# A 1 KB read of w_in on ScalarE's DMA queue at the start of an attention and feed-forward kernel

## The chip, the cores and the metric

The kernel runs on one NeuronCore of a Trainium2 chip, as one launch. Its time is device microseconds (us), lower is better. Five engines work side by side, each with its own instruction stream: TensorE (PE in the profile, with its weight loads as PEld), VectorE (DVE), ScalarE (ACT), GpSimd (POOL) and SyncE (SP). Transfers between the chip's main memory and SBUF are done by 16 DMA engines; an instruction on one of the five engines' queues starts each transfer, and "landing" is the moment at which all of it has arrived and whoever waits for it may go on.

## The reference

```python
def _attn_ref(x, state):                       # x 8x8x512x64, state 8x8x32x64
    scores = scale * x @ state^T ; a = softmax(scores) ; xread = a @ state
    scores2 = scale * state @ x^T ; a2 = softmax(scores2) ; sread = a2 @ x
    return concatenate([xread, sread], axis=2)
def _moe_ref(x, w_in, w_out):                  # 4608 rows of 512, w_in 512x2048, w_out 2048x512
    h = x @ w_in
    g = h - tanh(h)
    return g @ w_out
```

The output of the attention, 8 batches of 544 rows with the heads side by side, is the input of the feed-forward layer. Both weights come as 64-bit floating-point numbers and are turned into 32-bit ones on the chip.

## The kernel before

The heads' states are small (32 rows), so the kernel multiplies them into w_in ahead of time: for every batch and every head it forms state times w_in, and the hidden layer is then one product of the softmax weights with that. The 512 tokens of a batch and the 2048 hidden units are worked through in 16 steps of 128 hidden units per batch. One step is a product into a bank of PSUM (`hps`), tanh on ScalarE, subtraction on VectorE, a split into a high and a low part (ScalarE casts, VectorE subtracts), and the products with w_out into four banks (`ops`). This steady state makes up the time from about 60 us on.

Before it stands a start-up stage, in which the weights aren't there yet. It is written by hand: three strings list, for PE, DVE and ACT, the order of the steps by letters, and nothing on these engines may overtake. In it, the first batch's scores and softmax are computed, and each block of w_in, as soon as it has landed, is converted: `Weight.steps` (lines 146 to 161) gives for one block two shifts and masks on VectorE (L157, L158), a scaling copy on ScalarE (L160) and a last addition on VectorE (L161). Then `product` multiplies it with the states (L826).

A block of w_in or w_out is 128 rows of 4 KB, 512 KB in all, and `Weight.load` starts its transfer on SyncE's queue (L144; L135 for blocks that are kept in pairs). In DRAM the 16 blocks of w_in lie behind each other. The blocks are called `w00d`, `w01d`, `w02d` and so on as they land. The other inputs of the start-up lie in one array, `in_early`, which `fetch` (L657) takes piece by piece: `head` (states and a quarter of the tokens of the first heads, 384 KB), `xT00` (256 KB), `xT01` (512 KB), `sps` (256 KB), `sp4` (256 KB), `bdr1` (64 KB) and `xT1` (two of 512 KB).

All transfers of the kernel before are started by SyncE, in program order. Which come first is written out at L660 to L670: `head`, `xT00`, `w00d`, `xT01`, `sps`, `w01d`, `sp4`, `bdr1`, `xT1` twice, and then 14 weight blocks. Completions are counted on eight semaphores, which are called DMAHW0 to DMAHW7 and given out in turn; a transfer isn't started until the one eight places ahead, which used the same semaphore, has landed.

Of the kernel before, what the change touches and what calls it, by code (L numbers as in the profile page):

```python
# [10 lines left out]
U32 = mybir.dt.uint32  # L11
# [34 lines left out]
def attention_ffn(ctx: ExitStack, tc: tile.TileContext, early, xT, xn, bh, sm, sl, win, wout, xout, sout):  # L46
# [10 lines left out]
    nc = tc.nc  # L57

    cpool = ctx.enter_context(tc.tile_pool(name="cpool", bufs=1))
    pool = ctx.enter_context(tc.tile_pool(name="pool", bufs=2))  # L60
# [593 lines left out]
    def fetch(dst):  # L654
        nonlocal start
        n = dst.shape[-1]
        nc.sync.dma_start(dst, early[P * start : P * (start + n)].rearrange("(p n) -> p n", p=P))  # L657
        start += n

    fetch(head[:, :768])  # L660
    fetch(xb.rearrange("p c x -> p (c x)"))
    load(1)
# [481 lines left out]
```

## Time and profile before

| | us |
|---|---|
| median of 3 runs | 640.93 |
| lowest and highest run | 639.73 and 642.14 |
| span of the profiled execution, first to last instruction | 638.7 |
| PE busy in it | 631.7 (99%) |
| DVE busy in it | 438.4 (69%) |
| ACT busy in it | 353.6 (55%) |

For the profiled execution its span is known; the runs' median stands 2.2 us above it, which is what lies around the span and the spread of the runs. The profile gives for each instruction its engine, line, start and length, and for an idle stretch ahead of it what ended it. A DMA's own row (SPq) is the time in which the queue starts it, not the transfer.

### The profile page before, as it was taken

What the parts mean: (1) busy time and instruction counts of PE and PEld (TensorE: products, weight loads), DVE (VectorE), ACT (ScalarE), POOL (GpSimd) and SP (SyncE); (2) the same over time, 40 slices, a digit from 0 to 9 for tenths busy, and PEclk for the clock granted to TensorE, in tenths of its full rate; (3) what the DMA queues carried; (4) which work ended last, traced back from release to release, by engine and by line L of the source; (5) the groups of instructions that cost most, each with busy time, mean ns of one, the idle gap of its engine ahead of it and who ended that gap; (6) DMA issues with size and microseconds to landing.
All of it is one profiled execution on the core that took longest, in us unless ns stands there. A gap on an engine that the chain in (4) does not pass through costs nothing.

```text
span 638.7 us, 10135 instructions
## 1 busy us (share of the span) xinstructions
PE 631.7 (99%) x3772; PEld 502.4 (79%) x3772; DVE 438.4 (69%) x752; ACT 353.6 (55%) x639; POOL 0.3 (0%) x5
## 2 busy tenths in 40 slices
PE   8999999999999999999999999999999999999998
PEld 4476867888888788878888788878888788888887
DVE  5998898898683874688563678377764766464563
ACT  4966677787783443656553458254543453343553
POOL 0000000000000000000000000000000000000000
PEclk9999999999999999999999999999999999999999
DMA  8993897477885335543633236682463124221410
GB/s 331 401 304 116 316 352 244 139 241 233 247 258 155 104 99 201 172 137 107 196 113 105 79 111 208 209 308 83 136 194 90 35 83 148 76 66 34 132 34 33
DMA packets 66592, 105.84 MB, mean 166 GB/s; under 512 B 12272, under 2 KB 32368, under 8 KB 66544
## 3 DMA queue, kind: packets, MB, share of 16 engines
q1 hardware_dynamic: 66544, 105.21, 50.4%
q8 instruction: 29, 0.48, 0.3%
q14 instruction: 19, 0.16, 0.1%
HBM read 69.01 MB, written 35.65 MB: 164 GB/s over the span
## 4 chain that ended last, share of the span: by engine, by line
PE 94%; DVE 2%; DMA 2%; ACT 1%; issue 0%; SPq 0%; DVEq 0%
PE ops L566 19%; PE ops L567 19%; PE ops L568 19%; PE hps L513 8%; PE hps L515 8%; PE hps L514 8%; PE hps L498 2%; PE mps L249 2%; PE hps L887 1%; DMA w01d<-in_win 1%; PE mps L826 1%; PE rps L436 1%; PE sps L318 1%; PE hps L499 1%; PE mps L248 1%; PE ops L913 1%
## 5 line engine op out<-in xcount | busy, mean ns | idle before, releaser
L566 PE MATMUL ops<-wo,g 128*128 128x512 f32 x534 | 209.0, 393 | 0.0
L567 PE MATMUL ops<-wo,g 128*128 128x512 f32 x534 | 208.3, 390 | 0.0
L568 PE MATMUL ops<-wo,g 128*128 128x512 f32 x534 | 198.7, 390 | 0.0
L527 ACT ACTIVATE t<-hps 128x512 f32<-128x512 f32 (+1 forms) x119 | 70.7, 595 | 145.9 <-PE hps L515 143.0
L527 DVE TENSOR_TENSOR t<-hps,t 128x512 f32<-128x512 f32 (+1 forms) x119 | 81.4, 685 | 99.7 <-ACT t L527 99.2
L566 PEld LDWEIGHTS ops<-wo,g 128*128 128x128 f32 x534 | 100.3, 188 | 26.0 <-issue 2.9
L567 PEld LDWEIGHTS ops<-wo,g 128*128 128x128 f32 x534 | 100.2, 188 | 21.9 <-issue 1.3
L568 PEld LDWEIGHTS ops<-wo,g 128*128 128x128 f32 x534 | 99.8, 188 | 22.3 <-issue 0.8
L116 DVE TENSOR_TENSOR g<-t,g 128x512 fp32r<-128x512 f32 (+1 forms) x134 | 87.2, 655 | 33.6 <-ACT g L115 32.5
L115 ACT CAST g<-t 128x512 fp32r<-128x512 f32 (+1 forms) x134 | 79.6, 596 | 45.7 <-DVE t L527 39.2
L513 PE MATMUL hps<-aT,m 128*128 128x512 f32 x232 | 90.6, 391 | 0.0
L514 PE MATMUL hps<-aT,m 128*128 128x512 f32 x232 | 90.3, 389 | 0.0
L515 PE MATMUL hps<-aT,m 128*128 128x512 f32 x232 | 89.9, 390 | 0.0
L513 PEld LDWEIGHTS hps<-aT,m 128*128 128x128 f32 x232 | 43.5, 188 | 10.8 <-DVE w31r L158 0.8
L515 PEld LDWEIGHTS hps<-aT,m 128*128 128x128 f32 x232 | 43.5, 188 | 9.2
L514 PEld LDWEIGHTS hps<-aT,m 128*128 128x128 f32 x232 | 43.6, 188 | 8.9
L116 DVE TENSOR_TENSOR wst<-w,wst 64x512 fp32r<-64x512 f32 (+1 forms) x56 | 36.3, 648 | 8.1 <-ACT wst L115 6.5
L116 DVE TENSOR_TENSOR m<-mr,m 128x1024 fp32r<-128x1024 f32 x29 | 35.4, 1222 | 3.5 <-ACT m L115 3.0
L250 ACT COPY st<-mps 128x512 f32<-128x512 f32 (+1 forms) x56 | 30.2, 557 | 10.1 <-PE mps L249 6.8
L115 ACT CAST m<-mr 128x1024 fp32r<-128x1024 f32 x29 | 30.4, 1047 | 5.7 <-DVE mr L282 5.5
L115 ACT CAST wst<-w 64x512 fp32r<-64x512 f32 (+1 forms) x56 | 32.8, 585 | 0.7
L498 PE MATMUL hps<-srT,wm 128*128 128x512 f32 x60 | 21.7, 396 | 0.0
(232 smaller groups left out, 575.2 us busy)
## 6 DMA issues: line engine op xcount, KB each, us to landing
md<-st SPq DMA_DIRECT2D x96, 128.0 KB, 3.0
mr<-md SPq DMA_DIRECT2D x20, 512.0 KB, 4.1
xn<-in_xn SPq DMA_DIRECT2D x16, 512.0 KB, 6.1
out_x<-ob SPq DMA_DIRECT2D x30, 256.0 KB, 3.0
xT<-in_xT SPq DMA_DIRECT2D x12, 512.0 KB, 5.2
w<-wf SPq DMA_DIRECT2D x12, 512.0 KB, 4.1
pd<-pe SPq DMA_DIRECT2D x16, 256.0 KB, 2.3
p2t<-pd SPq DMA_DIRECT2D x64, 64.0 KB, 2.0
```

The source lines that it names most:

```text
L115: nc.scalar.copy(hi, src)
L116: return (sub or nc.vector).tensor_sub(lo, src, hi)
L249: nc.tensor.matmul(ps, s[:, 0, h], t[:, e], start=(g == 1), stop=True)
L250: nc.scalar.copy(stage[:, e], ps)
L498: nc.tensor.matmul(ps, mhi[k][:, cols], both, start=(k == 0), stop=False)
L513: nc.tensor.matmul(ps, mhi[k][:, cols], ahi[:, k], start=(k == 0), stop=False)
L514: nc.tensor.matmul(ps, mhi[k][:, cols], alo[:, k], start=False, stop=False)
L515: nc.tensor.matmul(ps, mlo[k][:, cols], ahi[:, k], start=False, stop=(k == 1))
L527: tanhs.append((nc.scalar.activation(t, ps, AF.Tanh).ins, nc.vector.tensor_sub(t, ps, t).ins))
L566: nc.tensor.matmul(o, g[:, 0, tok], wo[f][:, 0, cols], start=first, stop=False)
L567: nc.tensor.matmul(o, g[:, 0, tok], wo[f][:, 1, cols], start=False, stop=False)
L568: return nc.tensor.matmul(o, g[:, 1, tok], wo[f][:, 0, cols], start=False, stop=last).ins
```

## The change

One small transfer is added. It reads, from the first block of w_in (the one that lands as `w00d`), the first 64 bytes of each of the first 16 rows, which are 4 KB apart, into a tile of 16 partitions by 64 bytes. The tile, `touch`, is read by nothing. The instruction stands on ScalarE's queue, in the program ahead of all other transfers.

```diff
         nc.sync.dma_start(dst, early[P * start : P * (start + n)].rearrange("(p n) -> p n", p=P))
         start += n
 
+    touch = pool.tile([16, 16], U32, tag="touch", name="touch", bufs=1)
+    nc.scalar.dma_start(touch, win[0].bitcast(U32)[:16, :16])
+
     fetch(head[:, :768])
     fetch(xb.rearrange("p c x -> p (c x)"))
     load(1)
```

On ScalarE, at the start of the program, the row of instructions before is this; `s` is the copy of the first scores, `w00r` the scaled copy of the first weight block, and in brackets stand the semaphores waited for:

```order
0 L1139 UNCONDITIONAL_BRANCH [waits barrier_Pool_Activation_PE_DVE_SP_release]
1 L723 ACT_TABLE_LOAD
2 L723 COPY s_197<-sps_175 128x256 [waits DVE_49]
3 L724 COPY s_197<-spsb 128x256 [waits DVE_49]
4 L160 ACTIVATE w00r<-w00d 128x512 [waits DMAHW2_49]
```

And of the changed kernel:

```order
0 L1142 UNCONDITIONAL_BRANCH [waits barrier_Pool_Activation_PE_DVE_SP_release]
1 L661 DMA touch<-in_win 16x16
2 L726 ACT_TABLE_LOAD
3 L726 COPY s_199<-sps_177 128x256 [waits DVE_49]
4 L727 COPY s_199<-spsb 128x256 [waits DVE_49]
5 L160 ACTIVATE w00r<-w00d 128x512 [waits DMAHW3_49]
```

The new transfer stands ahead of the load of ScalarE's table, and it has taken the first of the eight semaphores, so that `w00d` now counts on the fourth.

On SyncE's queue, from its start to the first weight block that waits, before:

```order
1 L657 DMA head<-in_early 128x768
2 L657 DMA xT_128<-in_early 128x512
3 L144 DMA w00d<-in_win 128x1024
4 L657 DMA xT_129<-in_early 128x1024
5 L657 DMA sps<-in_early 128x512
6 L144 DMA w01d<-in_win 128x1024
7 L657 DMA sp_127<-in_early 128x512
8 L657 DMA bdr_125<-in_early 128x128
9 L657 DMA xT_130<-in_early 128x1024 [waits DMAHW0_49]
10 L657 DMA xT_130<-in_early 128x1024 [waits DMAHW1_49]
11 L144 DMA w02d<-in_win 128x1024 [waits DMAHW2_49]
```

And of the changed kernel:

```order
1 L657 DMA head<-in_early 128x768
2 L657 DMA xT_128<-in_early 128x512
3 L144 DMA w00d<-in_win 128x1024
4 L657 DMA xT_129<-in_early 128x1024
5 L657 DMA sps<-in_early 128x512
6 L144 DMA w01d<-in_win 128x1024
7 L657 DMA sp_127<-in_early 128x512
8 L657 DMA bdr_125<-in_early 128x128 [waits DMAHW0_49]
9 L657 DMA xT_130<-in_early 128x1024 [waits DMAHW1_49]
10 L657 DMA xT_130<-in_early 128x1024 [waits DMAHW2_49]
11 L144 DMA w02d<-in_win 128x1024 [waits DMAHW3_49]
```

The order of the transfers is the same. One wait is new: `bdr1` (bdr_125) is now started only once `touch` has landed. The later ones wait for the same transfers as before, on the next semaphore. On PE, DVE and POOL the order doesn't change.

## Rows read from the trace of the kernel before

**Rows 1.** Stretches: from:to us, length, busy time by engine, clock, DMA share, GB/s.

```profile
8.00:48.00 40.00, 37.34 (x523) 22.59 (x522) 39.53 (x67) 31.32 (x61) 0.00 (x0) 1.00 1.04 363
48.00:60.00 12.00, 11.57 (x73) 7.92 (x74) 11.10 (x18) 7.07 (x11) 0.00 (x0) 1.00 0.38 129
60.00:638.70 578.70, 575.70 (x3157) 467.51 (x3155) 386.18 (x667) 313.18 (x564) 0.00 (x0) 1.00 0.47 152
```

**Rows 2.** The chain that ended last, at the start: start us, us, what.

```profile
3.06 8.17 DMA w01d<-in_win
...
11.25 0.68 ACT w01r L160
```

**Rows 3.** Timeline of PE, DVE and ACT, first 10 us: start, us, engine, line, operation.

```profile
0.73 1.28 ACT L723 ACT_TABLE_LOAD   x1 [0.73 <-PEq L1130]
...
3.74 1.12 PE L707 MATMUL sps<-head 128*64 128x256 f32 x4
4.65 1.07 PE L718 MATMUL spsb<-xT,head 128*64 128x256 f32 x4
...
5.39 0.37 ACT L723 COPY s<-sps 128x256 f32<-128x256 f32 x1 [3.38 <-DVE e L733]
...
6.25 0.69 DVE L743 TENSOR_REDUCE m<-e 128x16 f32<-128x512 f32 x1
...
8.03 0.43 DVE L157 TENSOR_SCALAR w<-w00d 128x512 uint32<-128x512 uint32 x1 [1.10 <-DMA w00d<-in_win]
8.03 0.68 ACT L160 ACTIVATE w00r<-w00d 128x512 int32<-128x512 uint32 x1 [1.41 <-DMA w00d<-in_win]
...
9.32 1.08 PE L710 MATMUL sps<-xT,head 128*64 128x512 f32 x4 [1.27 <-DMA xT<-in_early]
```

**Rows 4.** Stretches of the first 8 us, columns as in the first group.

```profile
0.00:4.00 4.00, 3.12 (x8) 2.11 (x10) 0.00 (x0) 1.28 (x1) 0.30 (x5) 1.00 0.54 184
4.00:5.00 1.00, 1.00 (x6) 0.46 (x6) 0.09 (x1) 0.00 (x0) 0.00 (x0) 1.00 0.84 313
5.00:6.00 1.00, 1.00 (x5) 0.36 (x2) 0.59 (x2) 0.37 (x1) 0.00 (x0) 1.00 0.90 266
6.00:7.00 1.00, 1.00 (x4) 0.84 (x4) 0.90 (x2) 0.37 (x1) 0.00 (x0) 1.00 0.86 317
7.00:8.00 1.00, 1.00 (x5) 0.57 (x3) 0.00 (x0) 0.00 (x0) 0.00 (x0) 1.00 1.06 412
```

**Rows 5.** DMA issues: tiles, queue, count, KB each, median us to landing.

```profile
sr<-sx SPq DMA_DIRECT2D x32, 16.0 KB, 1.9
...
ob<-half SPq DMA_DIRECT2D x4, 256.0 KB, 3.0
...
w00d<-in_win SPq DMA_DIRECT2D x1, 512.0 KB, 6.4
...
smr<-in_sl SPq DMA_DIRECT2D x1, 256.0 KB, 3.0
```

**Rows 6.** Timeline of SyncE's queue: start us, us of starting the transfer, line.

```profile
0.73 0.39 SPq L657 DMA_DIRECT2D head<-in_early  x1
...
1.64 0.43 SPq L144 DMA_DIRECT2D w00d<-in_win  x1
...
4.29 1.25 SPq L657 DMA_DIRECT2D bdr<-in_early  x1
5.58 1.20 SPq L657 DMA_DIRECT2D xT<-in_early  x2
8.03 0.33 SPq L144 DMA_DIRECT2D w02d<-in_win  x1
9.29 0.33 SPq L135 DMA_DIRECT2D wo0d<-in_wout  x1
```

**Rows 7.** Timeline of ACT and DVE where the block wo2 has landed.

```profile
25.30 1.19 ACT L188 ACTIVATE wo2r<-wo2d 128x1024 int32<-128x1024 uint32 x1 [0.81 <-DMA wo2d<-in_wout]
25.45 0.68 DVE L186 TENSOR_SCALAR wor<-wo2d 128x1024 uint32<-128x1024 uint32 x1
```

## The prediction

> **What bounds the kernel now.** I first looked at the long stretches. From 60 us to the end PE is busy 575.70 of 578.70 us [rows 1]: nothing in there can be won by a small transfer at the start, but whatever makes that stretch begin earlier is won whole, since PE then simply has its work earlier. Ahead of it, from 8 to 48 us, VectorE is busy 39.53 of 40 us and PE 37.34 [rows 1]. So VectorE's list of steps, once it has begun at 8 us, runs almost without a gap, and a start that is earlier by some part of a us ends earlier by the same, unless one of its inputs isn't there. So the question is what starts that list and which inputs hold it.
>
> The chain of waits says what comes first: a transfer, w01d, which holds the chain from 3.06 us for 8.17 us, and then ScalarE's conversion of it at 11.25 us [rows 2]. The timeline shows the same one block earlier. VectorE ends the maximum at 6.25 + 0.69 = 6.94 us and then idles 1.10 us until w00d has landed, at 8.03 us; ScalarE waits 1.41 us for the same landing, and PE waits 1.27 us for xT01, which is the next in the queue, until 9.32 us [rows 3]. So the start-up is held by landings, and w00d is the first that is waited for.
>
> **Why w00d lands so late.** It is started at 1.64 us [rows 6] and takes 6.4 us to land [rows 5]. Is it only the bytes? To 4 us 4 x 184 = 736 KB (of 1000 bytes) came, to 5 us 1049, to 6 us 1315 [rows 4]. In the queue stand head, xT00 and w00d with 384 + 256 + 512 KB (of 1024), which is 1180. So as many bytes as these three have were in at 5 + 131 / 266 = 5.5 us. The same for head and xT00 (655): before 4 us, and PE works on xT00 at 4.65 us [rows 3], at most 0.9 us after its bytes. By that w00d would land at 6.4 us; it landed at 8.03. Some of the 16 engines were 1.6 us late with their share of it, while others were already at later transfers. And from 4 to 7 us the rate was 313, 266 and 317 GB/s, against 412 right behind [rows 4]: 99 + 146 + 95 = 340 KB less than at the full rate, or 340 / 412 = 0.83 us of all engines. Something stalls engines in that stretch. It may be the first reads of w_in; this is what a touch ahead could take away. It may also be load.
>
> **The change part by part.** *The instruction itself* stands ahead of the table load on ScalarE. No transfer of before is started there; on SyncE starting one took 0.33 to 1.25 us [rows 6], and I take 0.4. The table load now ends at 2.01 us, and ScalarE's next work is at 5.39 us after 3.38 us of idling [rows 3]. With 0.4 us, or even 1.25, nothing is late: cost zero, hidden by that idling.
>
> *The transfer* is 16 x 64 bytes, 1 KB beside the 736 KB of the first 4 us. Its nearest row is the 16 KB transfer, which lands after 1.9 us [rows 5]. If the first read of w_in is slow it could take as long as w00d, 6.4 us. So it lands between 2.6 and 7.1 us; I take 3, nearer to the small row.
>
> *The new wait* holds bdr1 on SyncE, and behind it both xT1 and the weight blocks from w02d on. bdr1 was started at 4.29 us [rows 6], after my 3 us, so the cover is 1.3 us. At the late end bdr1 starts at 7.1 us instead, but by 4.29 us transfers of 2.75 MB (all up to sp4) had been handed over and 0.8 MB had come [rows 4]; the remaining 1.9 MB takes 4.7 us at 412 GB/s, until 9 us, so the DMA engines don't run dry either. Cost zero at both ends. The later transfers wait for the same predecessors as before.
>
> *The gain* lies between nothing and what VectorE idles. If w00d landed at 6.4 us, VectorE could go on at 6.94 us rather than at 8.03: 1.09 us. But that isn't kept. At 25.30 us ScalarE has waited 0.81 us for wo2d, and VectorE takes the same block at 25.45 us [rows 7]. VectorE is thus only 0.15 us behind that landing: if its list comes 1.09 us earlier, it stands still there until wo2d is in. What passes is 0.15 us and whatever wo2d itself lands earlier. That is a matter of bytes, since the DMA engines are full from 7 us on (412 GB/s, share 1.06 [rows 4]; 1.04 as a mean of 8 to 48 us [rows 1]): if no stall of w_in's first reads is left, the bytes missing in w00d's own stretch come back, 99 + 0.49 x 146 = 171 KB or 0.41 us. So the gain is between 0 and 0.56 us. I take 0.3, the middle: there is a late w00d, which speaks for some gain, but no row that says that its lateness is a first read. The sum: 638.7 - 0.3 = 638.4 us of span, and 640.93 - 0.3 = 640.6 us.
>
> For the other side there is a row too: in_sl is first read by a transfer of 256 KB that lands after 3.0 us, and a read of 256 KB of an array that the kernel itself wrote shortly before (ob<-half) takes 3.0 us as well [rows 5]. There the first read costs nothing that can be seen.
>
> The Trainium skill has two places that speak against the change. *DMA: Bandwidth & Descriptors*, section "Issuing engines are not separate DMA queues", says that transfers started by ScalarE and SyncE run on the same 16 engines and interleave, so that a second queue saves only the time of starting. *HBM Reference*, section "Latency", gives an average access as 0.2 us and one under high load as 2 us; w00d's lateness of 1.6 us would by that be load, which a touch doesn't take away. By either the sum would be 640.9; no run so far tells these from a slow first read.
>
> **The rivals.**
>
> *Nothing moves.* The stall at 4 to 7 us is load, or 64 KB of addresses are too few to prepare a block of 512 KB, or the touch waits in the same engines in which head follows, so that the wait is only moved. w00d then lands at 8.03 us again, and the time is 640.9 us. For it speaks in_sl's row [rows 5], against it that the stall begins just as w00d's turn comes.
>
> *The whole stall goes.* Everything missing from 4 to 7 us comes back (0.83 us), wo2d lands by as much earlier and VectorE keeps 0.15 + 0.83 = 0.98 us: 640.0 us. Against it: a good part of the missing bytes falls in the time from 5.5 us on, when xT01 of another array is in turn.
>
> *The stall moves to the front, and it is slower.* The touch arrives at the 16 engines together with head. If the wait for w_in's first reads stops an engine, head's rows stand behind it. head comes first in the chain: PE begins at 3.74 us with it, and the maximum on VectorE ends at 6.94 us, with 1.09 us to spare before w00d [rows 3]. A delay of head decides from 1.09 us on. With the 1.6 us of w00d's lateness the maximum ends at 8.5 us, VectorE goes on 0.5 us later than now, and as its list has no gaps that stays: 641.4 us; with a late engine on w00d besides, 641.9.
>
> **How the numbers follow.** Forecast, a small gain of 0 to 0.6 us: 0.45. Nothing moves: 0.25. The whole stall goes: 0.12. The stall moves to the front: 0.13. Something else, of either sign: 0.05. The three runs of before lie 1.2 us to either side of their median, and the runs after will too, so that a median of few runs is uncertain by some 0.8 us. The range holds the first two cases with that, and half of the two others: 639.2 to 642.0 us. 0.5% is 3.2 us, about what a measurement of this kernel can tell from no change; none of the worked-out cases reaches it. Faster by over 0.5% 0.02, within 0.5% 0.95, slower 0.03.
>
> **What would show it.** Right: in the changed trace w00d is taken by VectorE before 8 us, down to 6.94; ScalarE still waits for wo2d near 25 us, longer than 0.81 us; from 4 to 6 us more than 313 and 266 GB/s; bdr1 started at about 4.3 us again. Nothing moves: 8.03 and 25.30 us stand again. Moved to the front: PE begins with head clearly after 3.74 us. Wrong altogether would be a gain or loss of 2 us or more; it would need a stall that these stretches don't show, or a wait late in the kernel that the touch's semaphore brings in.

## The result and the profile after

The changed kernel takes 646.65 us, the median of 6 runs (645.77 to 647.77); the kernel before took 641.34 us beside it (6 runs, 639.73 to 643.38). The ratio is 1.0093, with a 95% interval of 1.0078 to 1.0108: slower, by 5.3 us between the medians and 6 us by the ratio, and outside the predicted range of 639.2 to 642.0 us.

The head of the changed kernel's page: span, busy time of PE with its share and count, and the granted clock in 40 slices.

```profile
span 645.0 us, 10136 instructions
...
PE 638.5 (99%) x3772; PEld 502.5 (78%) x3772; DVE 438.5 (68%) x752; ACT 353.9 (55%) x639; POOL 0.3 (0%) x5
...
PEclk9999999999999999999999999999999999999999
```

The span is 6.3 us longer than before (638.7). PE still has 3772 matmuls, is still busy 99% of the time, and the granted clock is at the top in every slice, as it was before. So PE neither waits more (6.5 us of the span are idle, 7.0 before) nor is throttled. It is busy 6.8 us longer (638.5 for 631.7) with the same work.

**The start went as hoped.** First 10 us of the changed kernel: start, us, engine, line, operation, and in brackets the idle time ahead of it.

```profile
0.73 0.41 ACTq L661 DMA_DIRECT2D touch<-in_win  x1
1.18 1.28 ACT L726 ACT_TABLE_LOAD   x1 [1.18 <-PEq L1133]
...
3.92 1.12 PE L710 MATMUL sps<-head 128*64 128x256 f32 x4
4.01 0.43 SPq L657 DMA_DIRECT2D bdr<-in_early  x1
...
6.02 0.33 SPq L144 DMA_DIRECT2D w02d<-in_win  x1
6.42 0.69 DVE L746 TENSOR_REDUCE m<-e 128x16 f32<-128x512 f32 x1
6.69 0.66 ACT L160 ACTIVATE w00r<-w00d 128x512 int32<-128x512 uint32 x1
7.03 0.42 DVE L157 TENSOR_SCALAR w<-w00d 128x512 uint32<-128x512 uint32 x1
```

SyncE starts w02d once w00d has landed, so its row tells the landing: 6.02 us, where it was 8.03 [rows 6]. VectorE takes w00d at 7.03 us without an idle stretch ahead of it, where it had idled 1.10 us [rows 3]. The DMA issues (tiles, queue, count, KB, us to landing) say the same: w00d takes 4.4 us instead of 6.4 [rows 5].

```profile
w00d<-in_win SPq DMA_DIRECT2D x1, 512.0 KB, 4.4
...
touch<-in_win ACTq DMA_DIRECT2D x1, 1.0 KB, 2.5
```

Two later points of the same timeline are wo2's conversion, which ScalarE had begun at 25.30 us and VectorE at 25.45 [rows 7], and the six products on which PE works near 57 us.

```profile
24.53 1.18 ACT L188 ACTIVATE wo2r<-wo2d 128x1024 int32<-128x1024 uint32 x1 [1.13 <-DMA wo2d<-in_wout]
24.54 0.69 DVE L186 TENSOR_SCALAR wor<-wo2d 128x1024 uint32<-128x1024 uint32 x1
...
56.34 2.74 PE L890 MATMUL hps<-at,mr 128*128 128x512 f32 x6
```

The same six products of the kernel before:

```profile
57.38 2.73 PE L887 MATMUL hps<-at,mr 128*128 128x512 f32 x6
```

At 57 us the changed kernel is 1.04 us ahead. From there to its end it takes 645.0 - 56.34 = 588.7 us, where the kernel before took 638.7 - 57.38 = 581.3. So 7.3 us (unrounded) are lost in the part that the prediction had set aside as one in which nothing can be won, with PE always busy.

**Where they are lost.** PE's costliest groups of the changed kernel: line, operation, tiles, shape, count; then busy us, mean ns of one, and idle time ahead.

```profile
L566 PE MATMUL ops<-wo,g 128*128 128x512 f32 x534 | 210.5, 396 | 0.0
L567 PE MATMUL ops<-wo,g 128*128 128x512 f32 x534 | 209.9, 393 | 0.0
L568 PE MATMUL ops<-wo,g 128*128 128x512 f32 x534 | 199.8, 392 | 0.0
L513 PE MATMUL hps<-aT,m 128*128 128x512 f32 x232 | 91.4, 394 | 0.0
L514 PE MATMUL hps<-aT,m 128*128 128x512 f32 x232 | 91.1, 393 | 0.0
L515 PE MATMUL hps<-aT,m 128*128 128x512 f32 x232 | 91.0, 394 | 0.0
```

And the same six of the kernel before:

```profile
L566 PE MATMUL ops<-wo,g 128*128 128x512 f32 x534 | 209.0, 393 | 0.0
L567 PE MATMUL ops<-wo,g 128*128 128x512 f32 x534 | 208.3, 390 | 0.0
L568 PE MATMUL ops<-wo,g 128*128 128x512 f32 x534 | 198.7, 390 | 0.0
L513 PE MATMUL hps<-aT,m 128*128 128x512 f32 x232 | 90.6, 391 | 0.0
L514 PE MATMUL hps<-aT,m 128*128 128x512 f32 x232 | 90.3, 389 | 0.0
L515 PE MATMUL hps<-aT,m 128*128 128x512 f32 x232 | 89.9, 390 | 0.0
```

Every one of them is 2 to 4 ns longer. That is under 1% of one, but (3 + 3 + 2) x 534 = 4.3 us and (3 + 4 + 4) x 232 = 2.6 us: 6.8 of the 7.3 us. Matmuls overlap and their ends are modelled, so the starts are the surer witness. One stretch of 18 products without a gap, its first and its nineteenth row, before:

```profile
216.05 0.39 PE L566 MATMUL ops<-wo,g 128*128 128x512 f32 x1
...
220.13 0.39 PE L566 MATMUL ops<-wo,g 128*128 128x512 f32 x1
```

and in the changed kernel:

```profile
216.79 0.40 PE L566 MATMUL ops<-wo,g 128*128 128x512 f32 x1
...
220.95 0.40 PE L566 MATMUL ops<-wo,g 128*128 128x512 f32 x1
```

4.08 us against 4.16: 227 ns from start to start, and now 231. Over the whole trace, counting some 2110 steps from one product of these six groups to the next behind it, the mean step is 226.8 ns before and 229.8 after. No wait, no clock and no order explains this. The same instructions on the same data run a little slower through the steady state, because of a 1 KB transfer in the first 4 us, or of something that came with it.

What came with it is an address. `touch` is a tile: it takes 64 bytes of each partition of SBUF, from byte 73344 on. In the two built programs 207 of the tiles that both have stand where they stood (the first half of w_out, g and four of the eight aT among them), and the 596 tiles that follow lie 64 bytes further: the raw weight blocks, the second half of w_out, m, t and all else. The prediction counted the instruction, the transfer and the wait, and not these bytes.

### The profile page after: what moved, and what is told of

Its sections match the earlier page's. It is cut to its first block, busy times and chain, and to the rows that moved or that the text cites. A ratio compares the mean times of both kernels' runs of the same rounds, so it can differ in the third digit from the quotient of the medians.

```text
span 645.0 us, 10136 instructions
## 1 busy us (share of the span) xinstructions
PE 638.5 (99%) x3772; PEld 502.5 (78%) x3772; DVE 438.5 (68%) x752; ACT 353.9 (55%) x639; POOL 0.3 (0%) x5
## 4 chain that ended last, share of the span: by engine, by line
PE 90%; DMA 5%; DVE 3%; SPq 1%; issue 1%; ACT 0%; ACTq 0%; DVEq 0%
PE ops L566 18%; PE ops L567 18%; PE ops L568 18%; PE hps L513 8%; PE hps L515 8%; PE hps L514 8%; PE hps L498 2%; DMA wo2d<-in_wout 2%; PE mps L249 2%; DMA xn<-in_xn 1%; DMA xT<-in_early 1%; PE rps L436 1%; PE hps L499 1%; PE sps L318 1%; PE mps L248 1%; DMA wn<-wf 1%
```

## The experiments

Two theories to begin with. **A, the addresses**: the 64 bytes push tiles that PE reads, and their new places make PE's products slower; the transfer itself is worth a small gain. **B, the transfer**: its queue, its semaphore or the earlier start makes the later work slower, by whatever way. All kernels compute the whole result. Edits are shown against the changed kernel where they keep the touch, against the kernel before where they do not.

**The touch without its tile.** The same transfer lands in 16 columns of `head` that nothing uses, so no tile moves.

```diff
-    touch = pool.tile([16, 16], U32, tag="touch", name="touch", bufs=1)
-    nc.scalar.dma_start(touch, win[0].bitcast(U32)[:16, :16])
+    nc.scalar.dma_start(head[:16, 768:784].bitcast(U32), win[0].bitcast(U32)[:16, :16])
```

> The same transfer of 16 x 64 bytes on ScalarE's queue, but into the unused columns 768 to 783 of the tile head, so that no tile of SBUF lies elsewhere than in the kernel before. Theory A (the 64 bytes of the tile touch push 56 later groups of tiles by 64 bytes, and that slows PE's matmuls): the matmul means go back to those of before (L567 390 ns, not 393), the earlier start stays, w00d is taken near 7.0 us, about 640.3 us or 0.999 of before. Theory B (the transfer or the second queue itself slows PE, or the earlier start does): the time of the changed kernel again, about 646.6 us, 1.008 to 1.011 of before.

Measured: 640.42 us, 0.999 of the kernel before (0.9972 to 1.0008). PE's groups:

```profile
L566 PE MATMUL ops<-wo,g 128*128 128x512 f32 x534 | 209.0, 393 | 0.0
...
L513 PE MATMUL hps<-aT,m 128*128 128x512 f32 x232 | 90.6, 391 | 0.0
```

393 and 391 ns, as before the change. The transfer, its queue and its semaphore are all there, and the loss is gone.

**The tile without the touch.** No transfer, but a tile of the same size in the same place (GpSimd clears it once, in the first microseconds).

```diff
+    pad = pool.tile([16, 16], U32, tag="pad", name="pad", bufs=1)
...
+    nc.gpsimd.memset(pad, 0)
```

> No transfer is added. A tile of 16 x 64 bytes that GpSimd sets to zero is put where touch stood, so that the same tiles are pushed by 64 bytes and nothing else changes. Theory A (addresses): matmul means as in the changed kernel (L567 393 ns), w00d taken at 8.0 us as before, about 647.6 us, 1.009 to 1.012 of before. Theory B (transfer, queue or earlier start): 641.3 us, 0.998 to 1.002.

Measured: 647.3 us, 1.0103 (1.0076 to 1.013). PE's groups:

```profile
L566 PE MATMUL ops<-wo,g 128*128 128x512 f32 x534 | 210.6, 396 | 0.0
...
L513 PE MATMUL hps<-aT,m 128*128 128x512 f32 x232 | 91.3, 394 | 0.0
```

396 and 394 ns, as in the changed kernel. So these two runs settle between A and B: the whole loss comes from 64 bytes that nothing uses, and none of it from the transfer. B falls. The parts also make up the whole, within their intervals: 1.0103 x 0.999 = 1.0093.

**Twice the distance.** The touch's tile gets 128 bytes, in case only a multiple of 128 is wanted (in before all the large tiles begin at 128 modulo 512 bytes). To make room, it shares the buffer of a later tile, m110; the tiles between the two move by 128 bytes, the last ones in SBUF stay.

```diff
-    touch = pool.tile([16, 16], U32, tag="touch", name="touch", bufs=1)
-    nc.scalar.dma_start(touch, win[0].bitcast(U32)[:16, :16])
+    touch = pool.tile([16, 32], U32, tag="m2p", name="touch", bufs=1)
+    nc.scalar.dma_start(touch[:, :16], win[0].bitcast(U32)[:16, :16])
```

> The touch into a tile that takes 128 bytes of each partition instead of 64 (the tile shares the buffer of the later tile m110, for which there would be no room otherwise). All tiles between the two are pushed by 128 bytes. Theory A in the form that the boundary counts (before, nearly every tile began at a multiple of 128 bytes, after at 64 more): as before, matmul mean of L567 390 ns, about 640.3 us. Theory A in the form that it is only a matter of which tiles lie at which distance from the unmoved ones: slower again, 644 to 648 us. Theory B: 646.6 us.

Measured: 649.58 us, 1.0149 (1.0115 to 1.0183). It is worse, not cured. If the distance matters, it is by a longer period than 128 bytes.

**The same 64 bytes further on.** The pad is allocated later, just ahead of `blank` and so behind m, so that what PE reads in its main products stays; t, sm, e, the output tiles and others are pushed.

```diff
+    pad = pool.tile([16, 16], U32, tag="pad", name="pad", bufs=1)
...
+    nc.gpsimd.memset(pad, 0)
```

> No transfer is added. A tile of 16 x 64 bytes, set to zero by GpSimd, is put ahead of the tile blank, so that only the later tiles are pushed by 64 bytes: t (what VectorE and ScalarE work on between the products), sm, e, wf, ob, stage. What PE reads in the steady state, g, aT, aT0, m and w_out, stays where it was. If PE's own reads are what is slowed: 641.3 us, 0.998 to 1.002. If VectorE's and ScalarE's accesses at the pushed addresses disturb PE: 644 to 647.6 us. Theory B: 641.3 us.

Measured: 642.01 us, 1.0011 (0.9997 to 1.0025). PE's main groups and those of line 248 and 249, where a pushed tile (sms) meets one that is not (wst):

```profile
L567 PE MATMUL ops<-wo,g 128*128 128x512 f32 x534 | 208.5, 390 | 0.0
...
L513 PE MATMUL hps<-aT,m 128*128 128x512 f32 x232 | 90.6, 391 | 0.0
...
L249 PE MATMUL mps<-wst,sms 128*128 128x512 f32 (+1 forms) x56 | 19.9, 378 | 0.0
...
L248 PE MATMUL mps<-wst,sms 128*128 128x512 f32 (+1 forms) x32 | 11.6, 368 | 0.0
```

The two lines in the kernel before:

```profile
L249 PE MATMUL mps<-wst,sms 128*128 128x512 f32 (+1 forms) x56 | 19.7, 374 | 0.0
...
L248 PE MATMUL mps<-wst,sms 128*128 128x512 f32 (+1 forms) x32 | 11.4, 362 | 0.0
```

The main products keep their pace; the few whose two tiles now lie 64 bytes differently to each other run 4 and 6 ns longer (0.4 us of the whole). Pushing the tiles that only the other engines read and write costs next to nothing: the interval ends at 1.0025, and the mean step of the main products is 227.1 ns for 226.8. That led to a finer question: is it the place of a tile relative to the other (**C**), or the address itself (**D**)?

**All tiles pushed alike.** The pad stands ahead of the first tile, so that all move by 64 bytes together.

```diff
+    pad = cpool.tile([16, 16], U32, name="pad")
     wop = [cpool.tile([P, 2, 2, DM], F32R, name=f"wo{f}") for f in range(0, NFF // 2, 2)]
...
+    nc.gpsimd.memset(pad, 0)
```

> No transfer is added. The 64 bytes stand ahead of all tiles, so that w_out's first half, g, aT and all the others are pushed by the same 64 bytes and no two tiles move against each other. In the kernel before every large tile begins at 128 modulo 512 bytes of its partition. Theory C (what counts is where the tiles that PE reads at the same time, weights and moving data, lie relative to each other): 641.3 us, 0.998 to 1.002, L567 390 ns. Theory D (what counts is where a tile begins in itself, 128 modulo 512 being good and 192 bad): 647 us or more, since now all of PE's reads are at 192.

Measured: 640.04 us, 0.9988 (0.9976 to 1.0001). C stands and D falls: what costs is that some tiles moved and others did not.

**256 and 512 bytes.** Pads of these sizes stand where the touch stood; to make room for them the later tiles bdr, which lay near the end of SBUF, take the buffer of bdr1, which lies near its start. (The edit for 256; 512 has `[16, 128]`.)

```diff
-    bdr1 = pool.tile([P, 4, NS], F32, tag="bdr1", name="bdr1", bufs=1)
+    bdr1 = pool.tile([P, 4, NS], F32, tag="bdr", name="bdr1", bufs=1)
...
+    pad = pool.tile([16, 64], U32, tag="pad", name="pad", bufs=1)
...
+    nc.gpsimd.memset(pad, 0)
```

> No transfer is added. 256 bytes stand where touch stood (bdr1 and the later bdr share a buffer, which makes the room). Tiles from there on begin at 384 modulo 512, the ones ahead of it at 128. If 512 bytes or more is the period (C or D): slower, 644 to 650 us (64 bytes gave 647.3, 128 bytes 649.6). If the period is 256 or less: 641.3 us; after 64 and 128 bytes were both slow it is no less than 256.

> No transfer is added. 512 bytes stand where touch stood, with the same sharing of bdr. If the period is 512 bytes or a part of it (C or D): 641.3 us, 0.998 to 1.002, L567 390 ns. If only the exact places of before are good, or the period is longer than 512: 644 to 650 us.

Measured: 640.48 us, 1.0003 (0.9985 to 1.002) with 256 bytes, and 640.59 us, 0.9998 (0.9983 to 1.0012) with 512. Neither costs anything that can be told from noise. That all large tiles of before agree modulo 512 bytes had made 512 the other candidate; 256 is enough. With 128 bytes slow and 256 free, the sizes tried fit a period of 256.

**Only m pushed.** The pad is allocated just ahead of m's buffers, so that of the main products' tiles only m moves; g and both halves of w_out stay.

```diff
+            if self.name == "wo6":
+                pads.append(pool.tile([16, 16], U32, tag="pad", name="pad", bufs=1))
...
-    m_first = {}
+    m_first, pads = {}, []
...
+    nc.gpsimd.memset(pads[0], 0)
```

> No transfer is added. The 64 bytes stand ahead of the two buffers of m, so that w_out's second half (slots) and aT0 stay and, of what PE reads in the steady state, only m, the weights of the hidden layer's products, is pushed (and the later tiles, which cost nothing in pad64_late). If moving data must be pushed for a loss: 641.3 to 642 us. If weights pushed against moving data do it as well: 643 to 647 us, L513 to L515 slower than 391, 389 and 390 ns.

**All but m pushed.** The 64 bytes stand where the touch stood, and 192 more (`back`, allocated where the pad of the last kernel was) bring m and what follows to 256; bdr1 shares a buffer as above.

```diff
+                pads.append(pool.tile([16, 48], U32, tag="back", name="back", bufs=1))
...
+    pads.append(pool.tile([16, 16], U32, tag="pad", name="pad", bufs=1))
```

> No transfer is added. 64 bytes stand where touch stood and 192 more ahead of m, so that m and all later tiles lie 256 bytes on, and only parts, aT0, twins and slots are pushed by 64. In the steady state PE reads from these w_out's second half and, in batches 3, 5 and 7, aT0, both as moving data, against weights (g, m) that stand where they were or 256 on. If only m pushed against the rest costs: 640.4 us. If any pair pushed costs: 643 to 647 us, with the ops products of hidden units 1024 to 2047 slower.

Measured: with m alone pushed 647.43 us, 1.0099 (1.0074 to 1.0124); with all but m 645.39 us, 1.007 (1.0054 to 1.0087). PE's groups with m alone pushed (the code has two more lines, so 568 is the 566 of before):

```profile
L568 PE MATMUL ops<-wo,g 128*128 128x512 f32 x534 | 209.8, 395 | 0.0
L569 PE MATMUL ops<-wo,g 128*128 128x512 f32 x534 | 209.3, 392 | 0.0
...
L515 PE MATMUL hps<-aT,m 128*128 128x512 f32 x232 | 92.0, 397 | 0.0
L516 PE MATMUL hps<-aT,m 128*128 128x512 f32 x232 | 91.8, 396 | 0.0
```

and with all but m:

```profile
L568 PE MATMUL ops<-wo,g 128*128 128x512 f32 x534 | 210.7, 396 | 0.0
L569 PE MATMUL ops<-wo,g 128*128 128x512 f32 x534 | 209.0, 391 | 0.0
...
L515 PE MATMUL hps<-aT,m 128*128 128x512 f32 x232 | 91.5, 395 | 0.0
L516 PE MATMUL hps<-aT,m 128*128 128x512 f32 x232 | 90.7, 391 | 0.0
```

With m pushed the products that read m are the worst hit, 6 to 7 ns longer than the 391 and 389 of before. But those of w_out and g, whose own two tiles kept their places, are 2 ns longer too. Either move alone costs most of the loss, and the two do not add up: both together are pad64's 1.0103. The second kernel had been expected to slow the products with w_out's second half. They did lose more, but not alone: told apart by the order of the built program, the mean step grew by 2.1 to 2.9 ns for the four tiles of the second half, which were pushed, and by 1.2 to 1.8 ns for the four of the first, which were not.

So it is not only the distance between a product's own two tiles. Where the others are slow can be read from the trace of the kernel with m alone pushed: right behind the products that read m. One row of twelve products of w_out, its first, its seventh, and the product of m behind its twelfth:

```profile
217.57 0.39 PE L568 MATMUL ops<-wo,g 128*128 128x512 f32 x1
...
218.96 0.39 PE L568 MATMUL ops<-wo,g 128*128 128x512 f32 x1
...
220.32 0.40 PE L515 MATMUL hps<-aT,m 128*128 128x512 f32 x1
```

The first six take 1.39 us, 232 ns each; the last six take 1.36 us, 227 ns each as before. It is the same over the whole trace. The first six products of w_out behind one of m have a mean step of 231.1 ns (538 steps), the next six one of 226.6 (401 steps); in the kernel before these are 226.8 and 226.7. The products of m themselves have 233.2, for 227.0. Behind the products of sms and wst, of which sms is pushed and wst is not, it is alike: the first six have 230.4 ns (159 steps) for the 227.2 of before, the next six 226.6. So in this kernel the loss sits in the products whose own two tiles moved against each other and in the six behind them. With all but m pushed, few products are so far behind one with moved tiles (89 steps from the seventh to the twelfth), and they are not back at the old pace: 229.5 ns. Why the loss reaches on, no run shows.

**32 bytes**, as a pad where the touch stood:

```diff
+    pad = pool.tile([16, 8], U32, tag="pad", name="pad", bufs=1)
...
+    nc.gpsimd.memset(pad, 0)
```

> No transfer is added. 32 bytes stand where touch stood. If every distance that is no multiple of 256 bytes costs: 644 to 650 us (64 gave 647.3, 128 gave 649.6 with the touch). If 64 bytes are the smallest step that counts: 640.4 us.

Measured: 649.32 us, 1.0125 (1.0108 to 1.0143). Slow as well: of 32, 64, 128, 256 and 512 bytes only the last two cost nothing.

**The touch, with its tile a multiple of 256 bytes, and again in head**, both with more runs:

```diff
-    bdr1 = pool.tile([P, 4, NS], F32, tag="bdr1", name="bdr1", bufs=1)
+    bdr1 = pool.tile([P, 4, NS], F32, tag="bdr", name="bdr1", bufs=1)
...
-    touch = pool.tile([16, 16], U32, tag="touch", name="touch", bufs=1)
-    nc.scalar.dma_start(touch, win[0].bitcast(U32)[:16, :16])
+    touch = pool.tile([16, 64], U32, tag="touch", name="touch", bufs=1)
+    nc.scalar.dma_start(touch[:, :16], win[0].bitcast(U32)[:16, :16])
```

> The changed kernel with its tile touch made 256 bytes wide instead of 64 (bdr1 and the later bdr share a buffer, which makes the room); the transfer is the same 16 x 64 bytes. By the theory that PE's tiles must not be moved against each other by less than 256 bytes: matmul means of before (L567 390 ns), about 640.3 us, 0.997 to 1.001. If the touch's own landing in a tile of its own slows PE: 646.6 us.

> The touch into unused columns of head once more, in more rounds, to size what the touch itself gives: it took 0.999 of before (0.9972 to 1.0008). By the sum of the prediction: 0.3 us less than before, ratio 0.9995. If the whole of the earlier start were kept (1.1 us): 0.9983. If the touch does nothing: 1.000.

Measured: 639.97 us, 0.9981 (0.9971 to 0.9991) with the tile of 256 bytes, and 640.3 us, 0.9988 (0.9978 to 0.9998) in head. Both intervals end below 1: with the distances kept, the touch comes out 0.1 to 0.2% ahead of the kernel before. That is likely a gain, but these times alone don't show it: pad64_all, which has no touch, also came out at 0.9988 (0.9976 to 1.0001).

## Why the prediction was wrong

**The step that failed** is in the part "The change part by part". It takes the edit apart into an instruction, a transfer, a wait and a gain, and the first three held; the gain had the right sign. The fifth part, 64 bytes of SBUF ahead of 596 tiles, has no line in it, and it alone is worth more than all others: pad64, which is that part and nothing else, measures 1.0103. The first paragraph prepared the mistake. It read from [rows 1] that PE is busy 575.70 of 578.70 us, and concluded that nothing can be won there by a small transfer. That is so, but a stretch in which PE never waits is also the one in which a slower PE costs in full, as a mean of 3 ns on each of some 2300 products (1602 + 696) does. The last paragraph named a loss of over 2 us as the sign of being wrong altogether, and looked for its cause in a stall or a late wait. It was neither: a few waits of the start-up changed by less than 1 us, and PE's idle time as a whole fell, from 7.0 to 6.5 us.

A rule on addresses was kept throughout. The Trainium skill, *SBUF — State Buffer*, section "Operand start alignment", wants an operand to start at a multiple of its element size and says of itself that it is about legality, not speed. Every tile here starts at a multiple of 4 bytes in all the kernels, and their pace still differs by 1% with the distances between the tiles.

**The other steps**, in their order:

- *The instruction*: 0.41 us for the 0.4 taken. The table load moved to 1.18 us, and ScalarE still idled 3.11 us ahead of its next work. Cost zero, as said.
- *The transfer*: it landed after 2.5 us, at 3.2 us, near the 3 taken and far from the late end of 7.1.
- *The new wait*: bdr1 was started at 4.01 us, not later than the 4.29 of before [rows 6]. Cost zero, as said.
- *Why w00d lands late*: right that the lateness can be taken away. The stretch from 4 to 5 us sets the two kinds of kernel apart in every trace: 412 to 436 GB/s in the five with a touch, 262 to 348 in the nine without. In this pair the DMA engines moved 424, 340 and 383 GB/s from 4 to 7 us, for 313, 266 and 317 [rows 4]:

```profile
4.00:5.00 1.00, 1.00 (x6) 0.57 (x8) 0.00 (x0) 0.00 (x0) 0.00 (x0) 1.00 1.06 424
5.00:6.00 1.00, 1.00 (x7) 0.24 (x4) 0.51 (x2) 0.37 (x1) 0.00 (x0) 1.00 1.03 340
6.00:7.00 1.00, 1.00 (x5) 0.89 (x6) 0.97 (x2) 0.58 (x2) 0.00 (x0) 1.00 0.97 383
```

- *The gain, and what passes of it*: right in its mechanism. VectorE did win 1 us at w00d, and then wo2d's landing was the limit: ScalarE waited for it 1.13 us, longer than the 0.81 of [rows 7], and VectorE took the block 0.01 us behind ScalarE, where it had been 0.15. The size was taken as 0.3 us, between 0 and 0.56. In this pair of traces it is 0.77 us at wo2d and 1.04 us at 57 us, but a single trace of before is a poor measure: w00d lands late by a varying amount even with no edit that concerns it. In the nine traces without a touch it landed between 6.43 and 8.10 us, in the five with one (four kernels, one of them twice) between 5.91 and 6.44. wo2's conversion began at 25.02 us on average without and 24.69 with, and the six products near 57 us at 57.03 and 56.50: 0.33 to 0.53 us. The ratios of the last two runs stand for 0.8 and 1.2 us, with intervals that reach down to 0.1 and 0.6. The term was right in sign as far as the traces of the start-up tell; its size stays open between 0.3 and 1.2 us.
- *The rival that the stall moves to the front* came true at most in a harmless size. PE began with head at 3.92 us instead of 3.74 in this pair; over all the traces it was 3.74 to 3.90 us without a touch and 3.84 to 4.04 with one. The maximum ended at 7.11 us instead of 6.94, well within the 1.09 us to spare.
- *The rival that nothing moves*, for which the Trainium skill spoke with *DMA: Bandwidth & Descriptors*, "Issuing engines are not separate DMA queues": by it the touch, with its tile out of the way, would give a ratio of 1. The measured 0.9981 (0.9971 to 0.9991) and 0.9988 (0.9978 to 0.9998) differ from that by little, the second by no more than pad64_all without a touch. What the runs add is in the traces: with a small early read on the second queue, the big one behind it landed at the early end each time. Whether the two queues run on the same engines, no run here tests.

**What stays open.** Why the period is 256 bytes; why products whose own two tiles did not move against each other become slower as well, in the kernel with m alone pushed the six behind those that read m; and whether the touch helps because it is a first read of w_in or only because something is read early. No run touched another array or another part of w_in, or placed the read on SyncE's own queue, so the last is not known.

## What to carry to other kernels

When an edit adds a tile, however small, compare the addresses of all the other tiles before and after, above all where the engine that bounds the kernel never waits. In this kernel three ways cost nothing that stood out of the noise: the small tile in unused columns of one that is there, behind the tiles that the main products read, or as a multiple of 256 bytes. And when a kernel comes out slower though its bounding engine idles no longer than before, compare the mean time of one instruction of the largest groups: 3 ns of 390 was the whole answer here.

## What the runs showed of the hardware

That PE's pace depends on where its tiles lie to each other in a partition was new to me. At a granted clock of 0.999 or 1.0 in every trace, the products of 128x512 in fp32 had a mean step of 226.8 ns in the kernel before, and the same with the tiles pushed by 256 or 512 bytes, with all of them pushed alike, and with the touch in head or in a tile of 256 bytes. With a part of them pushed it was 229.8 ns for 64 bytes, 230.5 for 32 and 230.6 for 128. The ratio was 1.0125 with a part pushed by 32 bytes, 1.0103 by 64, 1.0149 by 128 (with the touch), 1.0003 by 256, 0.9998 by 512, and 0.9988 with all of them pushed alike by 64. So it is distances between tiles that decide, not the addresses by themselves, and the five sizes fit a period of 256 bytes. With m's tiles alone pushed, the products of m had 233.2 ns, the six of w_out behind them 231.1, and the six after those 226.6.

The second surprise is the start of the kernel: with the same transfers ahead of it, the first weight block landed at 6.43 us in one kernel and at 8.10 in another, over nine traces, and in all five traces with a read of 1 KB on another queue ahead of it, it landed at the early end, by 6.44 us.
